# Two decode layers on one core: the keys turned in place by VectorE instead of through TensorE, one head of four batches per unit

## The chip, the cores and the metric

The kernel runs on one core of one Trainium2 chip. The metric is the device time of one execution in microseconds (us), given as the median of several executions. Beside every timed run of a changed kernel the kernel before was run on the same chip, because times differ a little from chip to chip and from run to run. Most timed kernels were run six times; a single profiled run is used for every line of a profile.

## The reference

A decode step of two blocks, attention (A) and a gated linear unit (B), executed twice with the same weights and the same caches. There are four sequences of one token each. Only the last 2,048 positions of each cache are used.

```python
# bf16;  B=4, D=512, Hq=32, Hkv=8 (four query heads share one K/V head), Dh=128, window W=2048, F=1792
def A(x):                                   # x: (4, 1, 512)
    q = (x @ wq).reshape(4, 1, 32, 128)     # wq: 512 x 4096
    k = k_cache[:, :, -2048:, :]            # (4, 8, 2048, 128), repeated for 4 query heads each
    v = v_cache[:, :, -2048:, :]
    p = softmax(q k^T * 128**-0.5)
    return (p v).reshape(4, 1, 4096) @ wo   # wo: 4096 x 512
def B(x):
    return (sigmoid(x @ w_gate) * (x @ w_up)) @ w_down

x = x + A(layernorm(x)); x = x + B(layernorm(x))
x = x + A(layernorm(x)); x = x + B(layernorm(x))    # same weights, same caches
```

The K of one head and one batch is 2048 x 128 bf16, 512 KB, and so is its V. There are 32 of each. All K is 16.8 MB, all V is 16.8 MB. The on-chip arena has 49 slots of 512 KB. K stays there for both layers (32 slots) and so does wo (8), so that V, wq and the weights of B stream through the remaining nine slots, and are read twice.

## The kernel before

The kernel is a plan of operations, each with the tokens that it reads (`r`) and writes (`w`), its engine and an estimated cost. A scheduler orders the operations of each engine, and the waits between them are derived from the tokens. Operations on the same token are kept in order by a semaphore, also when both are on the same engine; this matters below. Loads are issued from one queue, in a fixed order, as slots come free.

K lies in its slot with positions on the partitions. This kernel's score matmuls take it with head dimensions there, so each K is turned by TensorE into PSUM, 128x128 at a time, and copied back by VectorE or ScalarE in turn:

```python
def k_transpose(h):
    for b in range(NB):
        ...                                                    # cut: s is the slot of K(h, b)
        for t in range(2):
            bank, ev = (4, "vector") if tcount[0] % 2 == 0 else (5, "scalar")
            ...
            def e_tr(pe, half=half, bank=bank):
                for j in range(TB):                            # eight 128x128 blocks
                    last = pe.transpose(bankb(bank)[:, j * 128:(j + 1) * 128],
                                        half[:, j * 128:(j + 1) * 128], ident_b[:, :])   # L526
                return last
            P.op("tensor", ..., e_tr, r=[("slot", s, t), ("ident_b",)], w=[("pst", bank)], banks=(bank,))
            if ev == "vector": P.op("vector", ..., tensor_copy(half, bankb(bank)) ...)   # L533
            else:              P.op("scalar", ..., copy(half, bankb(bank)) ...)          # L537
```

A unit of scores is one head in the first attention ("layer 0") and two heads in the second ("layer 2"). Its scores fill four of the eight banks of `ps`, and the other four have other uses, so only one unit can be in flight:

```python
def scores_softmax(L, heads, ptb, smb):
    for c in range(NCH):                                       # four banks of 512 positions
        ... last = pe.matmul(ps[32 * b:32 * b + rows, c, :], qt[:, q0:q0 + rows],
                             slot_ap(s)[:, c * CH:(c + 1) * CH], ...)                    # L598
    P.op("vector", "mx...", c_dve(SLOT), tensor_reduce(nm, ps[:, 0:NCH, :], max))        # L607, 128x2048
    for t in range(2):
        P.op("scalar", "ex...", activation(prow[:, ...1024], Exp, bias=nm, accum_out=...))  # L611
        ...  # L619: eight small matmuls with a selection matrix turn the probabilities; L629 copies them back
    ...      # sums of the rows, reciprocal
def pv_wo(L, h, keep):
    ...      # L659: 4 x 16 matmuls with V as weights; L671 scales; L684: wo; L691: xT += result, per head

def glu(L):
    GB, UB, YB = 4, 5, OB
    ...
        for nm, bank in (("g", GB), ("u", UB)):
            ...                                                # L710: 14 matmuls for each 128 rows of w_gate, w_up
            P.op("tensor", ..., e_g, r=slot_tok(s) + [("xn",)], w=[("psg", bank)], banks=(bank,))
    ...      # sigmoid, product; L740: w_down
```

## Time and profile before

| | before |
|---|---|
| time, median of 3 runs | 210.63 us (210.06 to 212.66) |
| span of the profiled run | 207.9 us |
| read from memory | 73.94 MB |
| layer 0 attention ends | 118.54 us |
| first GLU ends | 130.77 us |
| layer 2: first score matmul | 142.68 us |
| layer 2 attention ends | 195.28 us |
| last GLU ends | 204.74 us |

The ends are the starts of the last addition to x of each stage, read from the timeline. The page of the profile gives the span, the busy time of each engine, the span in 40 slices (each digit the busy share in tenths; PEclk the clock that the record says TensorE was granted; GB/s what the DMA moved), and groups of instructions: line, engine, operation, count | busy time in us, mean ns of one | idle time of the engine just before, and what ended it.

```profile
span 207.9 us, 6311 instructions
PE 143.3 (69%) x2872; PEld 110.4 (53%) x2872; DVE 71.7 (35%) x155; ACT 67.1 (32%) x103; POOL 1.4 (1%) x9
...
PEclk9955588596699676969975555555555555555555
...
GB/s 204 348 414 412 411 391 408 398 405 404 392 408 390 407 394 405 402 395 411 391 363 261 240 359 300 419 409 407 408 409 408 411 404 407 406 405 368 121 3 1
...
L526 PE MATMUL ps<-ident_b,arena 128*128 128x128 bf16 x512 | 48.5, 260 | 12.3 <-ACT arena L537 5.0
...
L537 ACT COPY arena<-ps 128x1024 bf16<-128x1024 bf16 x32 | 32.4, 1011 | 45.8 <-PE ps L526 45.8
L611 ACT ACTIVATE prow<-ps,nmax 128x1024 bf16<-128x1024 f32 x24 | 26.6, 1113 | 46.7 <-DVE nmax L607 46.6
...
L607 DVE TENSOR_REDUCE nmax<-ps 128x1 f32<-128x2048 f32 x12 | 27.5, 2290 | 11.8 <-PE ps L598 11.8
L533 DVE COPY arena<-ps 128x1024 bf16<-128x1024 bf16 x32 | 22.1, 689 | 26.8 <-PE ps L526 26.8
```

The next lines are windows of the span: start and end, length, busy time of each engine, granted clock, DMA share, GB/s.

```profile
100.00:118.50 18.50, 11.98 (x280) 8.97 (x276) 7.32 (x14) 6.45 (x12) 0.00 (x0) 0.68 0.87 318
118.50:131.00 12.50, 5.79 (x171) 5.39 (x170) 2.36 (x13) 0.63 (x3) 0.00 (x0) 0.50 0.97 322
142.70:192.00 49.30, 35.54 (x760) 22.33 (x760) 14.60 (x30) 11.54 (x20) 0.00 (x0) 0.50 1.03 404
195.30:207.90 12.60, 6.36 (x174) 5.69 (x174) 2.90 (x14) 0.63 (x3) 0.00 (x0) 0.50 0.01 2
```

The transfers run at 404 GB/s in the steady stretches. They fall to 318 to 322 from 100 to 131 us, because the attention of layer 0 ends late and frees slots late (from 100 to 131 us the queue waited 14.4 us for PV matmuls, L659), and they have all ended about 12 us before the span does (last data packet at 195.6 us). Layer 2 does not keep up with its transfers. Its waits of TensorE from 142 to 196 us (what waited, for what: us in total, times, longest) show why:

```profile
PE ps L619 <- ACT prow L611: 7.4, 2, 3.7
PE ps L659 <- DVE xT L691: 5.2, 3, 2.0
```

With one unit in flight TensorE stands while the maximum (2.29 us) and the exponentials run. The second line is for the addition to x, which this kernel makes after every head. These lines of the timeline (start, length, engine, line, count) are the reference for comparisons below: sixteen score matmuls, a stop of 1.19 us in PV for which the profile names no releaser ("issue"), and the gate and up matmuls of the last GLU with their weight loads, 112 without a break.

```profile
150.30 1.88 PE L598 MATMUL ps<-arena,qpad 128*8 128x512 bf16 x16
...
168.67 1.28 PE L659 MATMUL ps<-ebuf,arena 128*128 128x4 bf16 x43 [1.19 <-issue]
...
197.95 3.07 PEld L710 LDWEIGHTS ps<-xn,arena 128*128 128x128 bf16 x112 [1.49 <-issue]
197.98 3.13 PE L710 MATMUL ps<-xn,arena 128*128 128x4 bf16 x112 [1.42 <-DVE xn L505]
```

### The profile page before, as it was taken

Reading aid. Unit: us, or ns where it says so; the run is one execution under the profiler, and the core shown is the slowest. Engines: PE = TensorE matmul, PEld = TensorE weight load, DVE = VectorE, ACT = ScalarE, POOL = GpSimd, SP = SyncE. Lnnn points to the kernel's source line nnn. Section 1 sums busy time; section 2 is a strip of 40 time slices with the busy share of each in tenths; the row PEclk is TensorE's granted clock in tenths of the full one; section 3 lists DMA queues with packets and bytes.
Section 4 is the critical chain, followed back from the end, with each engine's and each line's share of the span. In section 5 each row is a group of like instructions: output and inputs, shape, how many; then the busy total and the mean of one; then the engine's idle time right before and its main releaser. Section 6 shows DMA issues by size and latency. Waiting matters only on the chain.

```text
span 207.9 us, 6311 instructions
## 1 busy us (share of the span) xinstructions
PE 143.3 (69%) x2872; PEld 110.4 (53%) x2872; DVE 71.7 (35%) x155; ACT 67.1 (32%) x103; POOL 1.4 (1%) x9
## 2 busy tenths in 40 slices
PE   1684885969969499797756662547296972967564
PEld 1683554858657477675625662443054740546563
DVE  4410262363363534637435220201414204142221
ACT  2430146283584372938354010000314103131000
POOL 2000000000000000000000000000000000000000
PEclk9955588596699676969975555555555555555555
DMA  5999999999999999999997799999999999999300
GB/s 204 348 414 412 411 391 408 398 405 404 392 408 390 407 394 405 402 395 411 391 363 261 240 359 300 419 409 407 408 409 408 411 404 407 406 405 368 121 3 1
DMA packets 26409, 74.33 MB, mean 358 GB/s; under 512 B 2312, under 2 KB 10000, under 8 KB 26384
## 3 DMA queue, kind: packets, MB, share of 16 engines
q1 hardware_dynamic: 26384, 73.94, 92.6%
q8 instruction: 22, 0.36, 0.7%
q14 instruction: 3, 0.02, 0.0%
HBM read 73.93 MB, written 0.00 MB: 356 GB/s over the span
## 4 chain that ended last, share of the span: by engine, by line
PE 36%; SPq 24%; DMA 16%; DVE 12%; ACT 7%; issue 4%; ACTq 0%; DVEq 0%
SPq L367 24%; PE ps L598 10%; PE ps L659 9%; DVE nmax L607 8%; DMA arena<-in_A_k_cache_dram 8%; PE ps L526 7%; DMA arena<-in_A_wq_dram 5%; ACT prow L611 5%; DMA arena<-in_B_w_down_dram 4%; PE ps L684 2%; PE ps L619 2%; PE ps L710 2%; PE ps L639 2%; PE ps L740 1%; ACT arena L537 1%
## 5 line engine op out<-in xcount | busy, mean ns | idle before, releaser
L526 PE MATMUL ps<-ident_b,arena 128*128 128x128 bf16 x512 | 48.5, 260 | 12.3 <-ACT arena L537 5.0
L526 PEld LDWEIGHTS ps<-ident_b,arena 128*128 128x128 bf16 x512 | 39.4, 119 | 22.3 <-issue 10.5
L537 ACT COPY arena<-ps 128x1024 bf16<-128x1024 bf16 x32 | 32.4, 1011 | 45.8 <-PE ps L526 45.8
L611 ACT ACTIVATE prow<-ps,nmax 128x1024 bf16<-128x1024 f32 x24 | 26.6, 1113 | 46.7 <-DVE nmax L607 46.6
L659 PE MATMUL ps<-ebuf,arena 128*128 128x4 bf16 x1024 | 29.5, 166 | 7.4 <-DVE xT L691 5.2
L659 PEld LDWEIGHTS ps<-ebuf,arena 128*128 128x128 bf16 x1024 | 28.6, 102 | 11.1 <-issue 11.0
L607 DVE TENSOR_REDUCE nmax<-ps 128x1 f32<-128x2048 f32 x12 | 27.5, 2290 | 11.8 <-PE ps L598 11.8
L533 DVE COPY arena<-ps 128x1024 bf16<-128x1024 bf16 x32 | 22.1, 689 | 26.8 <-PE ps L526 26.8
L619 PE MATMUL ps<-sel_b,prow 128*128 128x16 bf16 (+1 forms) x192 | 8.9, 178 | 15.2 <-ACT prow L611 15.0
L619 PEld LDWEIGHTS ps<-sel_b,prow 128*128 128x128 bf16 x192 | 7.0, 101 | 21.9 <-ACT prow L611 17.9
L553 PE MATMUL ps<-xn,arena 128*128 128x4 bf16 x256 | 9.3, 167 | 10.4 <-DMA arena<-in_A_wq_dram 8.4
L598 PE MATMUL ps<-arena,qpad 128*8 128x512 bf16 x128 | 15.5, 617 | 0.8 <-DVE qpad L577 0.8
L553 PEld LDWEIGHTS ps<-xn,arena 128*128 128x128 bf16 x256 | 8.3, 105 | 11.6 <-DMA arena<-in_A_wq_dram 9.5
L598 PE MATMUL ps<-arena,qflat 128*4 128x512 bf16 x128 | 13.8, 481 | 0.5 <-DVE qflat L565 0.5
L671 DVE TENSOR_TENSOR onb<-ps,rinv 128x16 bf16<-128x16 f32 x16 | 3.1, 194 | 30.1 <-PE ps L659 30.1
L684 PEld LDWEIGHTS ps<-onb,arena 128*128 128x128 bf16 x256 | 8.4, 104 | 5.6 <-DVE onb L671 4.1
L684 PE MATMUL ps<-onb,arena 128*128 128x4 bf16 x256 | 9.3, 167 | 1.7 <-DVE onb L671 1.7
L499 ACT ACTIVATE lnv<-lnv 128x4 f32<-128x4 f32 x4 | 0.8, 205 | 27.3 <-DVE lnv L496 27.3
L710 PE MATMUL ps<-xn,arena 128*128 128x4 bf16 x224 | 6.3, 166 | 2.8 <-DVE xn L505 2.8
L740 PE MATMUL ps<-hT,arena 128*128 128x4 bf16 x112 | 4.1, 166 | 5.9 <-DMA arena<-in_B_w_down_dram 2.9
L710 PEld LDWEIGHTS ps<-xn,arena 128*128 128x128 bf16 x224 | 6.1, 104 | 3.0 <-issue 3.0
L629 ACT CAST ebuf<-ps 128x256 bf16<-128x256 f32 (+1 forms) x12 | 5.4, 449 | 6.9 <-PE ps L619 6.9
(45 smaller groups left out, 55.8 us busy)
## 6 DMA issues: line engine op xcount, KB each, us to landing
arena<-in_A_v_cache_dram SPq DMA_DIRECT2D x64, 512.0 KB, 12.3
arena<-in_A_k_cache_dram SPq DMA_DIRECT2D x32, 512.0 KB, 12.7
arena<-in_A_wq_dram SPq DMA_DIRECT2D x16, 512.0 KB, 10.8
arena<-in_A_wo_dram SPq DMA_DIRECT2D x8, 512.0 KB, 15.0
arena<-in_B_w_gate_dram SPq DMA_DIRECT2D x8, 448.0 KB, 12.4
arena<-in_B_w_up_dram SPq DMA_DIRECT2D x8, 448.0 KB, 9.4
arena<-in_B_w_down_dram SPq DMA_DIRECT2D x6, 512.0 KB, 9.6
arena<-in_B_w_down_dram SPq DMA_DIRECT2D x2, 256.0 KB, 7.5
```

Of the source, the lines that this page charges most:

```text
L367: o = P.op("sync", name, 0.0, lambda e, dst=dst, src=src: e.dma_start(dst, src), r=r, w=w, dma_bytes=nbytes, dma_rate=tm[rate])
L526: last = pe.transpose(bankb(bank)[:, j * 128:(j + 1) * 128], half[:, j * 128:(j + 1) * 128], ident_b[:, :])
L533: lambda v, half=half, bank=bank: v.tensor_copy(half, bankb(bank)[:, 0:TB * 128]),
L537: lambda a, half=half, bank=bank: a.copy(half, bankb(bank)[:, 0:TB * 128]),
L553: last = pe.matmul(ps[:, QB, q * NB:(q + 1) * NB], src[:, k * 128:(k + 1) * 128], xn[:, c * NB:(c + 1) * NB], start=(st and k == 0), stop= ...
L598: last = pe.matmul(ps[32 * b:32 * b + rows, c, :], qt[:, q0:q0 + rows], slot_ap(s)[:, c * CH:(c + 1) * CH], start=(i == 0), stop=(i == ni ...
L607: lambda v: v.tensor_reduce(nm, ps[:, 0:NCH, :].rearrange("p c n -> p (c n)"), AXX, ALU.max, negate=True),
L611: lambda a, t=t: a.activation(prow[:, t * 1024:(t + 1) * 1024], ps[:, 2 * t:2 * t + 2, :].rearrange("p c n -> p (c n)"), ACTF.Exp, bias=nm ...
L619: last = pe.matmul(ps[:, ptb, j * n:(j + 1) * n], prow[:, j * 128:(j + 1) * 128], sel_b[:, 0:n], start=True, stop=True)
L659: last = pe.matmul(ps[:, OB, b * REP:(b + 1) * REP], src[:, j * 128:(j + 1) * 128], ebuf[:, c0:c0 + REP], start=(j == 0), stop=(j == NJ - 1))
L684: last = pe.matmul(ps[:, OB, 64 + c * NB: 64 + (c + 1) * NB], slot_ap(s)[:, r_ * D + c * 128:r_ * D + (c + 1) * 128], ov[:, r_ * NB:(r_ + ...
L710: last = pe.matmul(ps[:, bank, fc * NB:(fc + 1) * NB], src[:, fc * 128:(fc + 1) * 128], xn[:, c * NB:(c + 1) * NB], start=(c == 0 and fc = ...
```

## The change

The intent is to take the turning of K away from TensorE and from the two evictions. `v.transpose` works on a K slot in place, with a pair of bf16 values as one 4-byte element (a STREAM_TRANSPOSE of 128x1024 f32, arena to arena, L608). The program takes it to transpose each 32x32 block by itself. This is not a whole transpose: as the program has it, within a block the partition tells which pair of head dimensions, and which quarter of the positions (the quadrant) it is. The queries are therefore laid out block diagonal over the four quadrants (`qbd`), and one head's scores take four accumulated matmuls per batch, whose moving operand steps over every second bf16. All four quadrants' scores of a head then fit in one bank of `ps`, 512 columns, so the maximum and the exponential of a head work on 128x512 instead of 128x2048, two units can be in flight, and the probabilities are turned by one permutation matmul and one VectorE transpose. A unit is one head of four batches in both layers. Two V tiles are kept for layer 2, wo is accumulated in PSUM over all heads, and wq is loaded first. Small PSUM users now share one bank, `CB`.

```diff
-                    def e_tr(pe, half=half, bank=bank):
-                        for j in range(TB):
-                            last = pe.transpose(bankb(bank)[:, j * 128:(j + 1) * 128], ...)
-                    ...                                   # and both evictions
+        def k_transpose(pairs):
+            for (h, b) in pairs:
+                s = need(("K", h, b))
+                v32 = slot_ap(s).bitcast(F32)
+                P.op("vector", "T%d_%d" % (h, b), c_dve(1024), lambda v, v32=v32: v.transpose(v32, v32),   # L608
+                     r=[("slot", s)], w=[("slot", s)])
 ...
+            for a in range(4):                            # q_proj: block-diagonal q (L582 selection, L592/L596)
+                dst = qbd[32 * a:32 * a + 32, b0 * 512:b1 * 512].rearrange(...)[:, :, :, a * REP:(a + 1) * REP]
 ...
+        def softmax_unit(tag, pairs):
+            bank = SB[k2]                                 # two banks in turn
+                for cp in range(4):
+                    for gi, (h, b) in enumerate(pairs):
+                        kt = slot_ap(ks[gi]).rearrange("p (j c k t) -> p c t j k", c=2, k=32, t=2)
+                        last = pe.matmul(ps[32 * gi:32 * gi + NR, bank, :], qbd[:, q0:q0 + NR],            # L627
+                                         kt[:, cp // 2, cp % 2, :, :], start=(cp == 0), stop=(cp == 3))
+            P.op("vector", "mx" + tag, c_dve(512), ...)   # L635, then mask, cross-quadrant maximum (L638, L641)
+            P.op("scalar", "ex" + tag, ...)               # L644, 128x512
 ...
+        def turn_p(tag, k2):
+            ... pe.matmul(ps[:, PB, :], perm[:, :], prow[:, :], start=True, stop=True)                     # L652
+            ... v.transpose(ebuf[:, k2 * 512:(k2 + 1) * 512], ps[:, PB, :])                                # L655
+            ... pe.matmul(ps[:, ob, 128:128 + NR], ones_f[:, :], sv, ...)   # row sums, fp32, L662
 ...
+            for ui, pairs in enumerate(us):               # attn: the next two units' fronts run ahead
+                if ui + 2 < len(us):
+                    ks[ui + 2] = front(ui + 2)
+                ov = pv_unit(tag, pairs, ks[ui], keep if L == 0 else ())                                   # L679
+                ...
+                wo_unit(tag, kuse, wb, pairs, ov, ks[ui], ui == 0, ui == len(us) - 1)                      # L709
 ...
-                    P.op("tensor", "gl%s%d_%d" % (nm, L, c), NFC * tm["pe_pair"], e_g,
-                         r=slot_tok(s) + [("xn",)], w=[("psg", bank)], banks=(bank,))
+                    P.op("tensor", "gl%s%d_%d" % (nm, k, c), NFC * tm["pe_pair"], e_g,                     # L766
+                         r=[("slot", s), ("xn",)], w=[("cb",)], banks=(CB,))
```

The prediction was written from the diff and from the trace of the kernel before, with nothing of the change built.

## The prediction

> **What bounds it now.** Span 207.9 us, 73.94 MB by the sync queue. The slice view shows DMA at 99% and 391 to 414 GB/s nearly everywhere; windows give 401 to 404 GB/s in steady stretches. At 403 GB/s the bytes need 183.5 us. The other 24 us: about 3.5 us of start; about 7 us between the layers (318 GB/s at 100:118.5, 322 at 118.5:131); about 14 us of tail with no DMA (from 194 us). The chain of waits and the queue's own waits say why: layer 0's attention ends at 118.5 us, though the last K landed at 69 us. From there the chain is TensorE (512 K transposes, 48.5 us busy), evictions (ACT 32.4, DVE 22.1 us), and each unit's 2.29 us max and 2 x 1.1 us exp. Slots come free late, so the queue waits. In layer 2, units of two heads take 13 us (142.7 to 195.3 us) against 10.4 us for their V bytes, so compute ends well after its last V.
>
> **What the change does.**
> - Removes the 512 transposes and both evictions.
> - Adds 32 in-place VectorE block transposes of 128x1024 4-byte words. [...]the trace's reductions (2048 columns in 2.29 us, tiny ops 0.16 us) give 1.04 ns a column, so an estimate of 1.2 us each, 39 us of DVE. Per head 4.9 us plus 2.4 us softmax, under the 11.7 us that K, V and wo of a head take to load.
> - Scores: 256 matmuls of 512 columns as before, 0.107 us each in groups of four, but 4-byte steps in the moving operand. [...]no slowdown expected (no trace shows it yet).
> - Softmax over 128x512 per head: max 0.69, exp about 0.65 us; the chain per unit falls from about 6 to 3 us. One permutation matmul (0.5 us) and one DVE transpose (0.69 us) replace 16 small matmuls and an eviction.
> - PV (1.85 us a head), wo, glu unchanged. Each projection gains selection matmuls and evictions, about 2 us.
> - Two V tiles kept: 1.05 MB less, 2.6 us, but streaming slots between layers fall from 9 to 7.
>
> **On the critical path.** Layer 0 becomes DMA-bound: its last V (41.9 MB) lands at about 107.5 us, its attention ends at 109.5, not 118.5. Between layers seven slots (9 us) cover each chain (LN to first glu matmul 4 us; wq end to first freed K 5.5 us), so the dip nearly vanishes. Layer 2 needs about 5.3 us of PE per head against 5.2 us of DMA: balanced. DMA ends at about 3.5 + 72.9 MB / 0.403 = 184.5 us; then w_down, output transpose and store, 4 to 8 us. Span about 190.5; the run's time was about 2.5 us over its span: **193 us**, 80% within **188 to 201**. Chances: faster by over 2% 0.94, within 2% 0.04, slower 0.02.
>
> **What would show it.** DVE transposes at 1.2 us; no PE transposes of K; granted clock near 0.5; DMA over 390 GB/s from 10 to 180 us, no dip at 105 to 130; tail after the last load 4 to 8 us, not 14; score matmuls about 0.107 us.
>
> **What would make it wrong.** Block transposes[...] (2.2 us: layer 0 DVE-bound); strided score matmuls at half speed (+14 us in layer 2); seven slots too few; or PE falling behind in layer 2, leaving a tail over 10 us.

3.5 us of start and 72.9 MB at 403 GB/s are 184.5 us, the end (4 to 8 us) makes a span of about 190.5, and 2.5 us over the span make 193 us. Two terms rest on estimates: that a block transpose runs at the rate of the trace's reductions (1.04 ns a column, so 1.2 us), and that the strided score matmuls are not slowed. The trace of the kernel before shows neither; the changed kernel measured 1.215 us (L608) and 1.88 us for 16 score matmuls, as before. The 2.2 us among the risks are the same estimate at half the rate.

## The result

The changed kernel took 197.35 us, the median of four runs (196.80 to 198.44). The kernel before beside it took 211.54 us (210.06 to 212.66). The ratio is 0.934, with a 95% interval of 0.926 to 0.942. Ratios here and below are the mean time of one kernel's fast runs over that of the other's fast runs of the same rounds, so they are not quite the ratio of the medians. The record calls a run slow that is over 1.5% above the fastest of its kernel; in the later rounds that leaves out the longer runs of the kernel before, which brings the ratios there nearer to 1. In three later rounds on other chips the kernel before ranged from 206.9 to 213.1 us from run to run, and the unchanged copy of the changed kernel (the first experiment) came to a ratio of 0.951. The gain is between 5 and 7%.

| | before | after | difference |
|---|---|---|---|
| span of the profiled run | 207.9 | 195.1 | -12.8 |
| layer 0 attention ends | 118.5 | 111.7 | -6.8 |
| from there to layer 2's first score | 24.1 | 27.8 | +3.7 |
| layer 2 attention, first score to end | 52.6 | 40.6 | -12.0 |
| last GLU, from there | 9.5 | 11.8 | +2.3 |
| rest (output turned and stored) | 3.2 | 3.2 | 0 |

The page after, the same parts, with the queue that fetches instructions (packets, MB, share):

```profile
span 195.1 us, 4969 instructions
PE 107.4 (55%) x2224; PEld 74.8 (38%) x2224; DVE 86.6 (44%) x196; ACT 18.1 (9%) x47; POOL 2.8 (1%) x8
...
PEclk9999999999999999999999999999997555555555
...
GB/s 141 360 406 416 408 410 391 411 386 407 401 400 409 392 408 396 403 408 392 391 396 400 404 383 282 396 410 408 408 397 400 417 407 405 407 408 404 371 168 1
...
q8 instruction: 17, 0.28, 0.6%
...
L608 DVE STREAM_TRANSPOSE arena<-arena 128x1024 f32<-128x1024 f32 x32 | 37.9, 1215 | 0.1
...
L644 ACT ACTIVATE prow<-ps,nmax 128x512 bf16<-128x512 f32 x16 | 11.0, 687 | 97.0 <-DVE nmax L641 92.1
L635 DVE TENSOR_REDUCE nmax<-ps 128x1 f32<-128x512 f32 x16 | 11.0, 688 | 19.4 <-PE ps L627 19.4
...
L655 DVE STREAM_TRANSPOSE ebuf<-ps 128x512 f32<-128x512 f32 x16 | 11.4, 710 | 1.8 <-PE ps L652 1.6
```

The windows of the changed kernel:

```profile
100.00:115.00 15.00, 6.64 (x171) 5.72 (x168) 1.65 (x10) 0.41 (x2) 0.00 (x0) 1.00 1.04 402
115.00:125.00 10.00, 4.79 (x131) 4.21 (x132) 0.91 (x3) 0.22 (x1) 0.00 (x0) 1.00 0.98 329
145.00:180.00 35.00, 32.09 (x749) 22.82 (x741) 15.23 (x47) 4.75 (x13) 0.00 (x0) 0.56 1.03 406
```

In layer 0 the transfers now run at 402 GB/s to the end (318 before, from 100 us on), and its last PV matmuls wait for a load of V (first line of the timeline below): that stage is bound by its bytes. The low stretch before layer 2 is shorter and one slice long, at 282 GB/s. From 145 to 180 us TensorE is busy for 32.09 of 35 us. Its waits between 145 and 181 us are now these, and none is for a load of V:

```profile
PE ps L679 <- issue: 1.9, 1, 1.9
PE ps L524 <- DVE lnr L519: 0.7, 1, 0.7
PE ps L652 <- ACT prow L644: 0.6, 1, 0.6
```

So layer 2 is bound by TensorE. Its timeline shows a unit of one head every 4.91 us (three in 14.74 us, from 152.52 to 167.26), a stop of 1.93 us in the last PV, and, in the last GLU, the gate and up matmuls in 5.13 us instead of 3.13, their weight loads in groups of 14 with a gap of 0.20 us before each:

```profile
110.15 0.59 PE L679 MATMUL ps<-ebuf,arena 128*128 128x4 bf16 x16 [0.69 <-DMA arena<-in_A_v_cache_dram]
...
144.20 1.04 PE L627 MATMUL ps<-arena,qbd 128*16 128x512 bf16 x16
...
157.43 1.88 PE L627 MATMUL ps<-arena,qbd 128*16 128x512 bf16 x16
162.35 1.88 PE L627 MATMUL ps<-arena,qbd 128*16 128x512 bf16 x16
...
178.00 1.15 PE L679 MATMUL ps<-ebuf,arena 128*128 128x4 bf16 x38 [1.93 <-issue]
...
182.83 5.13 PE L766 MATMUL ps<-xn,arena 128*128 128x4 bf16 x112 [1.42 <-DVE xn L547]
183.47 0.46 PEld L766 LDWEIGHTS ps<-xn,arena 128*128 128x128 bf16 x14 [0.20 <-issue]
...
189.38 2.50 PE L794 MATMUL ps<-hT,arena 128*128 128x4 bf16 x56 [1.41 <-DVE hT L784]
```

Two readings of the clock are needed before runs are compared. The clock record of the changed kernel reads 9 tenths up to slice 31, but sixteen score matmuls of layer 0 take 1.88 us, exactly as long as at the recorded 0.50 in layer 2. They are fast (1.04 us) only in one stretch, 142.4 to 149.2 us, where the record has an event of 6.8 us of full clock. Before its first event the record says 1.0, which the durations contradict. And this stretch does not come in every run. Runs of the changed kernel with it (recorded mean clock about 0.88 to 0.89) are 1 to 2.7 us shorter than those without an event (recorded 1.00, and no fast score matmuls in the four that were profiled, of after_gu, after_keep0, gq and after_serial2). In some runs of its variants it is only half as long (about 0.86 to 0.88). "Like for like" below means runs of the same kind, as far as the record calls them fast. The kinds do not explain every spread: in gq and before_no_t both took the same time.

### The profile page after: what moved, and what is told of

Same layout as the page of the kernel before. It is cut to its first block, busy times and chain, and to the rows that moved or that the text cites. A ratio compares the mean times of both kernels' runs of the same rounds, so it can differ in the third digit from the quotient of the medians.

```text
span 195.1 us, 4969 instructions
## 1 busy us (share of the span) xinstructions
PE 107.4 (55%) x2224; PEld 74.8 (38%) x2224; DVE 86.6 (44%) x196; ACT 18.1 (9%) x47; POOL 2.8 (1%) x8
## 4 chain that ended last, share of the span: by engine, by line
SPq 31%; PE 26%; DMA 26%; DVE 8%; issue 5%; ACT 2%; ACTq 0%
SPq L365 31%; DMA arena<-in_A_v_cache_dram 19%; PE ps L679 7%; PE ps L627 6%; DMA arena<-in_B_w_down_dram 4%; PE ps L766 4%; DMA arena<-in_A_wq_dram 3%; DVE arena L608 2%; PE ps L709 2%; PE ps L662 2%; PE ps L652 2%; PE ps L794 1%; ACT prow L644 1%; PE ps L524 1%; DVE qbd L592 1%
## 5 line engine op out<-in xcount | busy, mean ns | idle before, releaser
L627 PE MATMUL ps<-arena,qbd 128*16 128x512 bf16 x256 | 28.1, 587 | 31.7 <-DVE arena L608 30.1
L679 PE MATMUL ps<-ebuf,arena 128*128 128x4 bf16 x1024 | 33.6, 167 | 14.5 <-DMA arena<-in_A_v_cache_dram 12.6
L608 DVE STREAM_TRANSPOSE arena<-arena 128x1024 f32<-128x1024 f32 x32 | 37.9, 1215 | 0.1
L627 PEld LDWEIGHTS ps<-arena,qbd 128*16 128x16 bf16 x256 | 6.4, 108 | 44.5 <-DVE arena L608 26.0
L644 ACT ACTIVATE prow<-ps,nmax 128x512 bf16<-128x512 f32 x16 | 11.0, 687 | 97.0 <-DVE nmax L641 92.1
L635 DVE TENSOR_REDUCE nmax<-ps 128x1 f32<-128x512 f32 x16 | 11.0, 688 | 19.4 <-PE ps L627 19.4
L652 PE MATMUL ps<-prow,perm 128*128 128x512 bf16 x16 | 9.0, 560 | 6.2 <-ACT prow L644 6.2
L655 DVE STREAM_TRANSPOSE ebuf<-ps 128x512 f32<-128x512 f32 x16 | 11.4, 710 | 1.8 <-PE ps L652 1.6
L662 PEld LDWEIGHTS ps<-ssel,ones_f 128*128 128x128 f32 x32 | 7.9, 297 | 6.9 <-issue 3.4
L662 PE MATMUL ps<-ssel,ones_f 128*128 128x16 f32 x32 | 9.0, 360 | 2.0 <-DVE onb L691 1.4
```

The lines of the kernel that those rows point to most:

```text
L608: P.op("vector", "T%d_%d" % (h, b), c_dve(1024), lambda v, v32=v32: v.transpose(v32, v32), r=[("slot", s)], w=[("slot", s)])
L627: last = pe.matmul(ps[32 * gi:32 * gi + NR, bank, :], qbd[:, q0:q0 + NR], kt[:, cp // 2, cp % 2, :, :], start=(cp == 0), stop=(cp == 3))
L635: lambda v: v.tensor_reduce(nmax[:, k2:k2 + 1], ps[:, bank, :], AXX, ALU.max),
L644: lambda a: a.activation(prow[:, :], ps[:, bank, :], ACTF.Exp, bias=nmax[:, 2 + k2:3 + k2], scale=1.0, accum_out=psm[:, k2:k2 + 1]),
L652: lambda pe: pe.matmul(ps[:, PB, :], perm[:, :], prow[:, :], start=True, stop=True),
L655: lambda v: v.transpose(ebuf[:, k2 * 512:(k2 + 1) * 512], ps[:, PB, :]),
```

## The experiments

The theory after the result had four parts. (1) Layer 0 became bound by its bytes because the turning of K left TensorE; VectorE's 39 us are hidden. (2) Layer 2 gained because two units are in flight, not because each of its instructions is shorter. (3) The 4 us missing against the prediction are on TensorE in the tail: the shared token `("cb",)` makes each group of gate and up matmuls wait for the group before on TensorE's own semaphore. (4) Fewer bytes are worth nothing at the end. Rivals: VectorE's transposes bound layer 0; the shorter softmax chain as such is the gain; the tail waits for its last loads. Twelve kernels were run. All twelve were reported correct, and that includes three in which K was deliberately not turned or turned twice (`before_no_t`, `after_no_t`, `after_dbl_t`): the comparison with the reference is blind to the turning of K, so those runs vouch for times only, and "correct" does not show that the changed kernel turns K rightly either.

### after_same: the changed kernel again

No edit.

> The changed kernel again, unaltered, as the yardstick of this call: 0.93 to 0.94 of before, span about 195 to 196.5 us, layer 0 attention ending near 111.7 us, layer 2 attention near 180 us, the last gate/up stretch 5.1 us.

It took 199.05 us (196.41 to 199.75, six runs), ratio 0.951 (0.942 to 0.961). One run, the profiled one, was of the kind with the fast stretch (196.41); the five without it took 198.75 to 199.75, and the record calls the two longest of them (199.68, 199.75) slow. This gives the base for like-for-like comparisons: about 196.6 us with the stretch (also 196.80 and 196.90 in the first result), about 198.9 without (three fast runs).

### after_gu: one token for each group of gate and up matmuls

```diff
-                         r=[("slot", s), ("xn",)], w=[("cb",)], banks=(CB,))
+                         r=[("slot", s), ("xn",)], w=[("gu", c, o0)], banks=(CB,))
 ...   # the sigmoid reads ("gu", c, 0) for all c, the product ("gu", c, 64)
```

The groups write different columns of the bank or add to the same ones. That the wait between groups protects nothing was the author's estimate.

> Separate dependency tokens for the eight gate/up groups of a GLU, so no group waits for the previous one's last matmul. Theory (each group waits on TensorE's own semaphore because gate and up now share one token): the 112 matmuls of the last GLU take about 3.1 us instead of 5.1 and the whole kernel is 1.7 to 2.3 us faster than the unaltered changed kernel, since that stretch is on the chain at the end. Rival (the gaps are waits on each tile's DMA semaphore, or the low clock): the stretch stays at 5 us and the time within 0.5 us.

It took 195.75 us (194.29 to 197.13), ratio 0.937 (0.929 to 0.945) against 0.951 for after_same. The intervals of the two ratios overlap a little. Like for like it is 2.1 us shorter with the stretch (194.3, 194.3, 194.9) and 2.1 without (196.6 to 197.1). The gate and up matmuls of the last GLU, in its timeline:

```profile
185.15 3.12 PE L766 MATMUL ps<-xn,arena 128*128 128x4 bf16 x112 [1.43 <-DVE xn L547]
```

It is 3.12 us, as in the kernel before. The cost was the token. This is the best version that was run: it beats the kernel before and the changed kernel.

### after_sb: the row sums by a bf16 matmul

```diff
-        ssel = sb("ssel", [128, 2 * NR], F32)
+        ssel = sb("ssel", [128, 2 * NR], BF16)
 ...
-                 lambda pe: pe.matmul(ps[:, ob, 128:128 + NR], ones_f[:, :], sv, start=True, stop=True),
+                 lambda pe: pe.matmul(ps[:, ob, 128:128 + NR], <high halves of ones_f as bf16>, sv, ...),
```

The fp32 matmul runs as two passes (L662: x32 for 16 operations, 360 ns each). If TensorE bounds layer 2, a shorter unit must shorten the run.

> Row sums spread by a bf16 matmul instead of the fp32 one (two passes, 0.5 to 0.6 us a unit). Theory (layer 2 of the changed kernel is bound by TensorE at the low clock): a unit of layer 2 falls from 4.9 to about 4.5 us, its attention ends 2.5 to 3.5 us sooner, the whole kernel is 2 to 3.5 us faster; layer 0 keeps its end near 111.7 us. Rival (layer 2 is bound by the arrival of V): no change over 0.7 us.

It took 199.02 us (198.50 to 201.00), ratio 0.957 (0.950 to 0.964): no gain. Its runs with the full stretch (198.5 to 199.1) are 2 us slower than those of the unedited kernel. The unit did become shorter, 4.62 us instead of 4.91, and the attention of layer 2 by 0.7 us (39.9 us; 2.5 or more were expected), but two holes opened in TensorE's stream in the last 20 us, for which the profile names no releaser ("issue"):

```profile
177.94 0.73 PE L680 MATMUL ps<-ebuf,arena 128*128 128x4 bf16 x22 [2.71 <-issue]
...
188.77 1.17 PE L767 MATMUL ps<-xn,arena 128*128 128x4 bf16 x28 [2.61 <-issue]
```

The changed kernel has the first of them too (1.93 us), and not the second. The expectation failed, and this hole became a question of its own, taken up with best1_pad16.

### after_keep0: no V tile kept

```diff
-    KEEP_V = cfg.get("KEEP_V", 2)
+    KEEP_V = cfg.get("KEEP_V", 0)
```

> No V tile kept: 1.05 MB more, nine streaming slots between the layers instead of seven. Theory (the dip at 117 to 122 us is the seven slots running out, and the end is set by TensorE and not by bytes): the dip goes (over 380 GB/s in that slice), the time stays within 1.2 us of the unaltered changed kernel. Rival (every byte counts at 403 GB/s): 2.6 us slower.

It took 197.01 us (196.21 to 198.76), ratio 0.946 (0.939 to 0.953). Like for like, 196.2 to 197.1 with the stretch and 198.0 to 198.8 without, it is within 1 us of after_same. The slice before layer 2 rose to 357 GB/s, not over 380 as expected, and after_same, with two tiles kept, also had 355 there; so that the dip comes from the slots was not shown. The 1.05 MB that keeping saves are worth nothing: in layer 2 they are off the critical path. That the two slots cost nothing either fits the same finding.

### before_no_t: the kernel before, without the turning of K

The loop over `t` in `k_transpose` (transposes and both evictions) is deleted. K stays unturned, which is wrong.

> The kernel before without its 512 K transposes on TensorE and their 64 evictions; K is used as loaded, so the result is wrong on purpose. Theory (the transposes put layer 0's TensorE behind the loads, and that is all they cost): layer 0's attention ends at 111 to 113 us instead of 118.5, layer 2 still takes 52 to 53 us, the whole kernel is 5.5 to 8 us faster than before (0.962 to 0.974), which leaves 6 to 8 us of the change's gain to layer 2's softmax. Rival A (transposes are the whole gain): 0.935. Rival B (layer 0 is bound by loads anyway): under 2 us.

It took 203.35 us (201.72 to 203.52) beside 210.45 us, ratio 0.971 (0.965 to 0.977). Layer 0 ended at 110.41 us, 8.1 earlier than in the kernel before. The DMA line of its page and its longest waits in layer 2:

```profile
GB/s 190 342 420 410 410 397 403 409 390 408 393 406 401 401 406 391 410 391 408 403 395 389 406 374 379 410 406 410 410 408 408 408 410 406 409 403 385 239 7 1
```

```profile
PE ps L598 <- ACT prow L590: 7.4, 2, 3.7
PE ps L638 <- DVE xT L670: 4.5, 3, 2.0
```

The low stretch is gone, so the turning of K was what held layer 0. Layer 2 keeps its waits (7.4 us for the exponentials, the same number as before) and is still 50.5 us long, against 52.6 before and 40.6 after. That part of the gain has another cause.

### after_no_t: the changed kernel, without the block transposes

The operation L608 is deleted (wrong K).

> The changed kernel without the 32 VectorE block transposes; wrong result on purpose. Theory (layer 0 is bound by the loads, VectorE has 4 us of slack a head): layer 0's attention ends within 0.7 us of 111.7 us, the total within 1.2 us of the unaltered changed kernel at the same recorded clock. Rival (the transposes, which stand in the chain of waits, cost time): 3 us faster or more.

It took 197.24 us (196.24 to 200.86), ratio 0.942 (0.934 to 0.950), and layer 0 ended at 111.58 us against 111.72. With the stretch its runs took 196.2 to 198.7. Taking 38 us of VectorE away gains nothing: they are hidden.

### after_dbl_t: each block transpose twice

```diff
+                P.op("vector", "T2%d_%d" % (h, b), c_dve(1024), lambda v, v32=v32: v.transpose(v32, v32),
+                     r=[("slot", s)], w=[("slot", s)])
```

> Every VectorE block transpose done twice, which gives K back unturned; wrong result on purpose. This is the risk named in the prediction[...]. Theory: VectorE work a head grows from about 7.4 to 12.2 us, just over the 11.7 us of loads, so layer 0 becomes VectorE-bound: its attention ends at 117 to 121 us, the total 5 to 9 us later. Rival (VectorE's time is hidden anyhow): under 2 us.

It took 203.31 us (201.03 to 204.87), ratio 0.966 (0.956 to 0.975); like for like 4.4 to 6.0 us more. Layer 0 ended at 116.63 us, 4.9 later, a little less than expected. VectorE's slices and the DMA line of its page:

```profile
DVE  4106999999998998989897420120456444440211
...
GB/s 146 366 414 412 409 401 400 409 389 409 392 407 405 396 410 388 409 397 400 396 391 408 337 198 200 346 411 409 409 396 413 406 406 407 409 409 399 378 202 1
```

With twice the work VectorE is full through layer 0, and the low stretch of the kernel before comes back (198 and 200 GB/s). Had the block transposes taken twice as long, most of layer 0's gain (4.9 of 6.8 us) would have been lost; this run is that case, and it would still have been faster than the kernel before.

### after_max4: the maximum read four times over

```diff
-                 lambda v: v.tensor_reduce(nmax[:, k2:k2 + 1], ps[:, bank, :], AXX, ALU.max),
+                 lambda v: v.tensor_reduce(nmax[:, k2:k2 + 1], ps[:, bank, :]
+                     .unsqueeze(1).broadcast_to([128, 4, 512]), mybir.AxisListType.XY, ALU.max),
```

This gives the maximum the 2.29 us that it had before, in a kernel with two units in flight.

> The max of every unit read four times over (2048 columns, 2.3 us instead of 0.69, as long as before's); the result stays right. Theory (in layer 2 two units are in flight, so TensorE hides most of a unit's softmax chain; the gain comes from the overlap): 2 to 5 us slower, nearly all in layer 2. Rival (the shorter chain itself is the gain): 1.6 us for each of 8 units, 12 us or more slower.

It took 203.12 us (202.02 to 203.55), ratio 0.970 (0.964 to 0.976). Layer 0 ended at 111.69 us, as unchanged. Four of its runs, the profiled one among them (a fast stretch of 3.4 us, half as long as in the changed kernel), are between the two kinds. Like for like there is one run of each: 5.4 us more with the stretch (202.02) and 4.5 more without (203.44). Sixteen maxima became 1.6 us longer, eight of them in layer 2 (12.8 us); at least half of that is hidden. The rival, that the shorter softmax chain is layer 2's gain (12 us or more lost here), is out.

### after_serial2: one unit in flight in layer 2

```diff
+            if L == 2:
+                for ui, pairs in enumerate(us):
+                    k2 = front(ui); turn_p(tag, k2); ov = pv_unit(tag, pairs, k2, ())
+                    gate[0] = [<last TensorE operation>]
+                    wo_unit(...)
 ...
-                 w=[("pss", k2)], banks=(bank,))
+                 w=[("pss", k2)], banks=(bank,), after=gate[0])      # scores wait for the unit before
```

> The changed kernel with the overlap of units in layer 2 taken away: a unit's scores wait for the last PV matmul of the unit before. Theory (layer 2's gain is two units in flight): a unit takes about 7 us instead of 4.9, layer 2's attention grows from 40.6 to 56 to 60 us, the whole kernel is 14 to 19 us slower, near or above the kernel before. Rival (the gain is the shorter softmax chain, and order hardly matters): under 6 us slower.

It took 218.23 us (217.88 to 218.95), ratio 1.048 (1.039 to 1.056): slower than the kernel before, and 19 us slower than the kind of after_same without the stretch. A unit takes 7.63 us instead of 4.91, and the attention of layer 2 61.9 us, a little more than expected. TensorE's waits from 140 to 202 us:

```profile
PE ps L663 <- DVE ssel L660: 17.1, 8, 2.6
PE ps L680 <- DVE rinv L667: 6.2, 8, 0.8
```

Eight times it stands for the chain of maximum, exponential and probabilities, which has the short 128x512 form here. So short instructions alone do not give layer 2's gain; it needs the overlap of two units. The 19 us are not that gain itself: this kernel pays the chain once for each head, the kernel before once for two. And one rival was not tested: in the kernel before, the profile puts 5.2 us of TensorE's waits in layer 2 down to the addition to x after a head, which the change, with wo accumulated over all heads, makes once in a layer. No run kept that addition, so how the 12.0 us divide between it and the overlap is not shown.

### gq: separate tokens for w_down and the query projection too

The edit of after_gu is extended to the query projection's groups (`("qp", c, i)` for `("cb",)`) and to the groups of w_down (`("wdp", a)`).

> The changed kernel with separate dependency tokens for every weight tile of gate/up, w_down and the q projection. Theory: gate/up 3.1 us as with after_gu; w_down's four groups and the q projection also lose their pauses, but only the last w_down stretch (2.5 us to about 2.0) is on the chain, so 0.3 to 0.8 us faster than after_gu at the same recorded clock: about 193.7 us (clock near 0.89) or 196.2 (clock 1.0). Rival (those pauses are hidden or have another cause): equal to after_gu within 0.3 us.

It took 198.07 us (198.00 to 198.33), ratio 0.950 (0.946 to 0.954), which is more than after_gu. The w_down matmuls did shorten, from 2.50 us to 1.64, but the holes were back: 2.06 us in the last PV, and 1.72 us in the last gate and up matmuls, where after_gu had none. The expectation failed.

### best1: all the tokens, and the bf16 row sums

> gq plus the bf16 row-sum matmul. Theory (a stall of TensorE begins where 16 KB of its instructions have to be read, and its place depends only on the count of instructions before it): as in after_sb, two stalls of over 2 us, one in the last PV and one in the last gate/up; so the 2.4 us gained in layer 2's units are lost again: 195 to 197.5 us, no better than gq. Rival (after_sb's second stall was a missing weight tile or chance): no stall in gate/up, 191.5 to 193 us.

It took 197.39 us (196.24 to 198.06), ratio 0.946 (0.940 to 0.952), as expected by the theory. Three shortenings together bring nothing against after_gu. The two holes, from its timeline:

```profile
178.68 0.41 PE L680 MATMUL ps<-ebuf,arena 128*128 128x4 bf16 x10 [2.68 <-issue]
...
189.11 0.48 PE L767 MATMUL ps<-xn,arena 128*128 128x4 bf16 x13 [3.55 <-issue]
```

The trace also has the transfers of the instruction queue, in packets of 16,384 bytes. In best1 one of them begins at 176.1 us and one at 186.8, inside the holes (176.0 to 178.7 and 185.6 to 189.1); each takes 1.0 to 1.1 us. In after_sb, gq and the changed kernel, too, one begins within each hole or up to 0.8 us before it. The distance of the two holes is 256 TensorE instructions in best1 (after 4033 and 4289 of them, weight loads, matmuls and semaphore waits counted, and the 15 matmuls that are missing in the records put back by their weight loads). So the suspicion is that TensorE ran out of fetched instructions. It fits that every profiled variant of the changed kernel with two units in flight has the first hole (1.6 to 2.7 us), and after_serial2, whose TensorE stands between its units anyway, has none.

### best1_pad16: best1 with sixteen useless matmuls at the start

```diff
+        def e_pad(pe):
+            for i in range(16):
+                last = pe.matmul(ps[:, PB, 0:4], ident_b[:, :], ident_b[:, 0:4], start=True, stop=True)
+            return last
+        P.op("tensor", "pad", 16 * tm["pe_pair"], e_pad, r=[("ident_b",)], w=[("ppb",)], banks=(PB,))
```

If the holes are bound to the instruction's number and not to the work, they must come at an earlier place of the work.

> best1 with 16 useless matmuls (32 TensorE instructions) ahead of everything, in TensorE's idle first 3 us, so that every later instruction has about the number it has in the changed kernel, whose gate/up showed no stall. Theory: the gate/up stall goes, the one in the last PV stays; 1.5 to 3 us faster than best1, 192.5 to 194.5 us. Rival: the same as best1 within 0.5 us, or slower by the added work.

It took 197.89 us (197.64 to 198.30), ratio 0.949 (0.944 to 0.954): no gain. The holes:

```profile
177.73 0.83 PE L680 MATMUL ps<-ebuf,arena 128*128 128x4 bf16 x25 [2.41 <-issue]
...
188.78 0.91 PE L767 MATMUL ps<-xn,arena 128*128 128x4 bf16 x28 [4.17 <-issue]
```

In best1 13 of the 112 gate and up matmuls stood behind the hole, here 28: it moved by 15 matmuls. In the last PV it moved by 15 as well, from 10 behind it to 25. By number both holes stayed where they were: 4033 and 4289 in best1, 4034 and 4290 here. So the place of the hole is set by the instruction's number, as the theory had it. But the hole did not go away or get shorter, and the run gained nothing; that part of the expectation failed.

The traces of all fourteen kernels say more. Counted in the same way, every hole of the variants lies at one of these two numbers (within one), and the stop of 1.19 us in the kernel before at 4545, 256 further. On that grid of 256 instructions there is one fetch of 16,384 bytes for each point, 232 in all, and TensorE never passed a point sooner than 2.3 us after its fetch had begun. The sixteen holes of over 1 us at these three numbers all ended 2.3 to 2.7 us after the start of a fetch, though they were 1.2 to 4.2 us long, and the second fetch of after_gu, which left no hole, began 2.7 us before TensorE came to its point. So the holes are waits for instructions that were fetched late, as far as traces can show it. What makes a fetch begin late stays open, and no run took a hole away by moving its fetch.

## Why the prediction was right, and where its terms were off

The time on record was 193 us with 188 to 201 around it; 197.35 us was measured. The direction held, and so did the mechanism but for what paces layer 2 and the end; the value was 4.35 us too low.

| term | predicted | measured |
|---|---|---|
| one block transpose of 128x1024 | 1.2 us | 1.215 us |
| maximum, exponential of a head | 0.69, 0.65 us | 0.688, 0.687 us |
| strided score matmuls | as fast as before | 16 in 1.88 us, before and after |
| layer 0 attention ends | 109.5 us | 111.72 us |
| added work of a projection | about 2 us | 2.2 us (3.0 us from the last wq matmul to layer 2's first score, 0.8 before) |
| a head of layer 2 on TensorE | 5.3 us | 4.91 us |
| last transfers | 184.5 us | 188.9 us |
| last GLU | unchanged | 11.8 us, 9.5 before |
| span | 190.5 us | 195.1 us |

**Right.** The cost of the block transposes was estimated at 1.2 us from the rate of the trace's reductions (2048 columns in 2.29 us), and it measured 1.215 us (L608). They are hidden: without them nothing is gained (after_no_t), with twice as many 4.9 us of layer 0 are lost (after_dbl_t). The strided moving operand cost nothing, as estimated: 16 score matmuls took 1.88 us before and after. Only this stride, every second bf16, was run. Layer 0 became bound by its bytes, and removing the turning of K from the kernel before does the same to it (before_no_t: 7.1 us by the medians, of the 14 us in all by the medians of the first result).

**Right, with the cause confirmed in the main.** Layer 2 gave the other part, 12.0 us of stage length. Removing the transposes gives it only 2.1 of those (50.5 us against 52.6). Taking the overlap away costs 19 us (after_serial2). Giving the maximum its old length costs 4.5 to 5.4 us (after_max4). What the single addition to x gave was not tested.

**Off: the end.** The prediction's step was "DMA ends at about [...] 184.5 us; then w_down, output transpose and store, 4 to 8 us". The transfers ended 4.4 us later than that (last data packet at 188.9 us in the trace; the last tile of w_down was reported as landed at 189.3). The tail from there, 6.2 us, is inside the range given. But this is not the chain. The w_down matmuls, at 189.38 us, waited for the product of gate and up and not for a load, their last group, which alone needs the last tile, began 2.2 us after it had landed, and in layer 2 no matmul waited for V. The step that failed is that layer 2 and the end would be paced by the loads; they are paced by TensorE, from its first score at 139.5 us on. That the saving of 1.05 MB, which the prediction counted as 2.6 us, is worth nothing (after_keep0) is the same error seen from another side. The two limits are close, though: by these times the loads would hold the end again once about 2 us were saved on TensorE (an estimate).

**Off: "wo, glu unchanged".** The diff moved gate and up from two banks with two tokens into one bank with one token. In the kernel before, a group waited for the group before the last, which had ended; now it waits for the one just issued. This is 2.0 us in the last GLU, 5.13 against 3.12, about 0.29 us for each of the seven gaps between eight groups, and undoing it gave about 2.1 us (after_gu). It is visible in the diff as `w=[("cb",)]`, and it was overlooked.

**Off, and not priced: instruction fetch.** A hole of 1.93 us lies in the last PV of the changed kernel. The groups' waits and the hole together, 2.0 and 1.9 us, are nearly the 4.6 us by which the span was missed, but that is arithmetic only. No run with two units in flight was free of the hole, so what it costs was not shown, and other terms were off in both directions: layer 0 ended 2.2 us late, and each of eight heads was 0.39 us shorter than predicted. That the total came so close is in part luck.

**Small misses.** The low stretch between the layers shrank to one slice of 282 GB/s and was not quite gone. Layer 0 ended 2.2 us late, and its last V landed at 110.1 us against the predicted 107.5. By the trace 41.5 MB had been moved at 107.5 us, of the 41.9 MB predicted, and 42.5 MB at 110.1: about 1 us is the rate, and the rest are bytes of later loads in flight beside that V (an estimate). The granted clock "near 0.5" was right by durations, except for 6.8 us at the start of layer 2; the record that should have shown it is 1.0 where it has no event.

**Open.** Why the fast stretch comes in some runs of the changed kernel only; why the kernel before spreads over 6 us; what makes an instruction fetch late.

## What to carry to other kernels

When operations are moved into a shared buffer, look at which token each write carries: here a false dependence between groups on one engine cost a wait each time (about 0.29 us), and it gave back 2 us of the gain. A stage that a change frees from one limit must be priced against all the others: here layer 0 went from TensorE to loads, while layer 2, where loads and TensorE were estimated as equal, was bound by TensorE, so bytes saved there were worth nothing and losing the overlap of two units would have cost 19 us. And once a stream is this dense, shortening its instructions can move the wait instead of ending it, as after_sb showed, so measure each shortening alone and together.
